# Attention, then two feed-forward layers: the attention's side work is laid into idle times behind its plan, and the change-over to the first layer is regrouped

## The chip, the cores and the metric

The kernel runs on one core of a Trainium2 chip. The metric is the device time of one execution in microseconds, the median of several runs. The engines are PE (TensorE, the matmuls), DVE (VectorE), ACT (ScalarE), POOL (GpSimd) and SP (SyncE, which here only issues DMAs). Each engine works through its own list of instructions in order, and waits on semaphores for the others.

## What is computed

```python
q_rot, k_rot = (rotate(q), rotate(k))          # rope; q, k, v: 4 batches, 8 heads, 576 tokens, 64
scores = scale * np.matmul(q_rot, k_rot.transpose(0, 1, 3, 2))
scores = scores - np.max(scores, axis=-1, keepdims=True)
attn = np.exp(scores)
attn = attn / (np.sum(attn, axis=-1, keepdims=True) + 1e-09)
x = np.matmul(attn, v)                          # -> 2304 tokens x 512
...
g = x @ w_gate                                  # MoE 1: 512 -> 1536
silu = g * (1.0 / (1.0 + np.exp(-g)))
val = x @ w_val
x = silu * val @ w_out                          # 1536 -> 512
...
h = x @ w_in                                    # MoE 2: 512 -> 2048
r = np.maximum(h, 0.0)
g = r * r
return g @ w_out                                # 2048 -> 512
```

## The kernel before

**Arithmetic.** Where full precision is wanted, an operand is split into a rounded high part and the remainder (two tiles or halves of a tile, `h` and `l`), and a product is three matmuls. The split is one ACT copy and one subtraction by DVE or POOL. The four batches' outputs x are 512 + 64 tokens each. MoE 1 does batches in pairs in the manner of Strassen: seven products of sums of blocks instead of eight. The sums of x blocks are called words (T1 to T4 are sums of two or more blocks, the others are plain x), and the sums of weight blocks are weight words.

**Attention** (up to some 355 us). 16 pairs of heads (4 batches, 4 pairs). For each: loads of q and k (`rot<-in_q_dram`), rope on DVE and POOL, copies to the layout of the heads (`kh`, `qa`, `qz` `<-rot`), scores `s` and their softmax (`nm`, `p`), transposes `pt` with copies `pc`, `av`, and then the output tile `xs`, which is split into `x0h`, `x0l` to `x3h`, `x3l` (one pair of names for each batch). Beside these lie *fillers*: the first two of MoE 1's chunks of ff columns for batches 0 to 2 (weights `w`, products `mm`, then `ys<-mm` by ACT and a store to `ypart` in DRAM).

The order of the attention is found by `Plan`: each operation is entered with its engine, its cost, a rank and what it reads and writes; a greedy loop with a clock of its own gives each engine that comes free the ready operation of the lowest rank. A tag has so many places, and an operation that begins a new buffer of the tag waits for a place. DMAs are operations on SP, with these two constants for when they land (ns, and bytes per ns):

```python
    LAND = 2000
    RATE = 310
```

In the plan lie also the spills (`xfull<-xs`, and `xsp<-x0h` and so on: the split x), and `add_words`: for the four words T1 to T4 of the first pair of batches it loads x back (`h<-xfull`, `wa<-xfull`), makes the sums (L777 and L778), stores them (`xsums`), loads each back (`h<-xsums`), splits it (L784 ACT, L785 POOL), and stores both halves (`xsum`).

**The change-over** (some 355 to 450 us). The order of everything after the attention is made by a second planner, `Order`, in stages. Stage 0 holds batch 3's part of the first two chunks (`q<-x3h`, L1064; then the 64 token rests of all batches, `xrh`, `xrd`, loaded by `accr<-xfull`), `down_first` (its products with `w_out`, `d<-h`, whose results go by `ys` and `yh` to `ypart[3]`), and the first weight words and x words of the steady state. `combine` loads raw weights, unpacks them (ACT, then three DVE instructions for each piece), adds them, and stores the words to `w1d` for later; `fetch_in` loads words stored before (`f<-w1d`), and `split_in` splits `f` into `wi`. The x words come by `xc<-xsp` and `xc<-xsum`. All of these DMAs are issued by SP.

Stage 1 is laid over the space of the attention's pools (`early.close()`); its tiles `cp`, `thr`, `th` are the copies by which ACT takes a product out of PSUM (`q` and `d`).

```python
    for o, ps, t in down_first(B - 1, hl):
        ys = new("ys")
        copy(ys, ps, 512, [t], [ys])
        dma(lambda o=o: ypart[B - 1][:, o, :], lambda ys=ys: ys(), [ys], [(ypd[B - 1], o)], 262144)
```

**Steady state** (from 450 us on). Two pairs of batches through MoE 1 and then MoE 2, PE busy nearly throughout; the change does not touch its code.

## Time and profile before

| | |
|---|---|
| median of 3 runs | 1140.83 us (1140.17 to 1141.53) |
| the profiled execution | 1141.04 us, its span 1139.3 us, mean granted clock 0.988 |
| PE | 1072.8 us busy (94%), 6126 matmuls |
| DVE, POOL, ACT | 738.2 us (65%), 703.8 us (62%), 612.1 us (54%) |
| DMA | 201.34 MB, mean 177 GB/s |

The busy time of an engine is the sum over its instructions. The span less PE's busy time, 66.5 us, is the time in which PE has nothing to do. Windows give the same by stretches of the program; the waits say for each engine who ended its idle times. In the timeline, the bracket behind an instruction is the idle time of its engine before it and who ended that. A granted clock of 1.00 is 2.4 GHz on PE.

### The profile page before, as it was taken

Reading aid. Unit: us, or ns where it says so; the run is one execution under the profiler, and the core shown is the slowest. Engines: PE = TensorE matmul, PEld = TensorE weight load, DVE = VectorE, ACT = ScalarE, POOL = GpSimd, SP = SyncE. Lnnn points to the kernel's source line nnn. Section 1 sums busy time; section 2 is a strip of 40 time slices with the busy share of each in tenths; the row PEclk is TensorE's granted clock in tenths of the full one; section 3 lists DMA queues with packets and bytes.
Section 4 is the critical chain, followed back from the end, with each engine's and each line's share of the span. In section 5 each row is a group of like instructions: output and inputs, shape, how many; then the busy total and the mean of one; then the engine's idle time right before and its main releaser. Section 6 shows DMA issues by size and latency. Waiting matters only on the chain.

```text
span 1139.3 us, 17496 instructions
## 1 busy us (share of the span) xinstructions
PE 1072.8 (94%) x6126; PEld 891.7 (78%) x6126; DVE 738.2 (65%) x1198; ACT 612.1 (54%) x1257; POOL 703.8 (62%) x596
## 2 busy tenths in 40 slices
PE   4898998999996949999999999999999999999998
PEld 3687787787884837888888888888888888788886
DVE  8676877666762617778866676575777756255454
ACT  7666767675652513654564455736554454553432
POOL 6877676678111505678858666785666669475651
PEclk9999999999999979999999999999999999999999
DMA  9876678899514753576668555454343435412102
GB/s 304 229 211 178 190 211 256 243 289 269 153 65 150 273 235 95 186 246 219 237 243 267 194 171 195 141 201 143 126 143 125 171 126 166 152 61 84 29 18 74
DMA packets 100824, 201.34 MB, mean 177 GB/s; under 512 B 17280, under 2 KB 43648, under 8 KB 100736
## 3 DMA queue, kind: packets, MB, share of 16 engines
q1 hardware_dynamic: 100048, 199.50, 54.3%
q8 instruction: 48, 0.79, 0.3%
q10 hardware_dynamic: 688, 0.72, 0.2%
q14 instruction: 40, 0.33, 0.1%
HBM read 116.98 MB, written 61.08 MB: 156 GB/s over the span
## 4 chain that ended last, share of the span: by engine, by line
PE 79%; DMA 9%; DVE 3%; SPq 3%; POOL 2%; ACT 2%; issue 1%; ACTq 0%; DVEq 0%; POOLq 0%
PE d L1064 36%; PE q L1064 26%; PE s L656 5%; PE av L719 5%; PE pt L685 4%; PE mm L820 3%; DMA qa<-rot 2%; DMA xc<-xsum 2%; DMA ypart<-ys 1%; SPq L636 1%; DMA v<-in_v_dram 1%; DMA h<-xfull 1%; POOL rot L566 1%; DVE nm L662 1%; DMA ypart<-yh 1%
## 5 line engine op out<-in xcount | busy, mean ns | idle before, releaser
L1064 PE MATMUL q<-xc,wi 128*128 128x512 f32 x1296 | 310.5, 392 | 16.7 <-ACT cp L930 16.2
L1064 PEld LDWEIGHTS q<-xc,wi 128*128 128x128 f32 x1296 | 242.5, 189 | 69.3 <-ACT cp L930 17.5
L915 POOL TENSOR_TENSOR wi<-f,wi 128x512 fp32r<-128x512 f32 (+1 forms) x144 | 167.1, 1176 | 70.2 <-ACT wi L914 64.5
L1064 PE MATMUL d<-wo,h 128*128 128x512 f32 (+1 forms) x870 | 199.9, 388 | 0.3 <-POOL h L915 0.3
L915 POOL TENSOR_TENSOR h<-th,h 128x512 fp32r<-128x512 f32 x104 | 136.2, 1336 | 101.0 <-ACT h L914 99.9
L1064 PEld LDWEIGHTS d<-wo,h 128*128 128x128 f32 x870 | 162.1, 188 | 34.8 <-POOL h L915 1.2
L919 DVE TENSOR_TENSOR acc<-d,acc 128x512 f32<-128x512 f32 (+1 forms) x193 | 132.1, 688 | 71.1 <-PE d L1064 66.8
L1064 PE MATMUL d<-h,wo 128*128 128x512 f32 (+1 forms) x600 | 126.1, 369 | 2.7 <-ACT wo L914 1.1
L656 PE MATMUL s<-kh,qa 128*128 128x288 f32 x320 | 104.2, 351 | 24.8 <-DVE qa L614 12.0
L1064 PEld LDWEIGHTS d<-h,wo 128*128 128x128 f32 x600 | 104.6, 188 | 23.1 <-POOL wo L915 1.6
L662 DVE TENSOR_REDUCE nm<-s 128x1 f32<-128x576 f32 x144 | 106.2, 751 | 23.5 <-PE s L656 22.4
L664 ACT ACTIVATE p<-s,nm 128x576 f32<-128x576 f32 x144 | 105.8, 736 | 27.1 <-DVE nm L662 24.7
L685 PE MATMUL pt<-ident,p 128*128 128x128 f32 (+1 forms) x720 | 109.5, 275 | 7.8 <-ACT pc L677 3.9
L915 POOL TENSOR_TENSOR wo<-wf,wo 128x512 fp32r<-128x512 f32 x52 | 68.0, 1307 | 78.9 <-ACT wo L914 41.4
L930 ACT ACTIVATE cp<-q 128x512 f32<-128x512 f32 x108 | 64.6, 599 | 83.5 <-PE q L1064 82.6
L914 ACT ACTIVATE wi<-f 128x512 fp32r<-128x512 f32 (+1 forms) x144 | 79.7, 572 | 49.2 <-POOL f L922 26.9
L685 PEld LDWEIGHTS pt<-ident,p 128*128 128x128 f32 (+1 forms) x720 | 85.9, 135 | 15.4 <-ACT pc L677 5.7
L919 DVE TENSOR_TENSOR q<-q,cp 128x512 f32<-128x512 f32 x36 | 25.2, 699 | 105.5 <-PE q L1064 104.5
L656 PEld LDWEIGHTS s<-kh,qa 128*128 128x128 f32 x320 | 61.3, 197 | 39.3 <-ACT p L664 20.2
L656 PE MATMUL s<-kl,qz 128*128 128x288 f32 x288 | 85.3, 304 | 0.0
L914 ACT ACTIVATE wo<-wf 128x512 fp32r<-128x512 f32 x52 | 32.9, 633 | 83.3 <-PE d L1064 70.2
L719 PE MATMUL av<-pc,v 128*64 128x256 f32 x640 | 77.5, 389 | 0.0
(167 smaller groups left out, 1837.7 us busy)
## 6 DMA issues: line engine op xcount, KB each, us to landing
raw<-in_moe_w_out_dram SPq DMA_DIRECT2D x26, 512.0 KB, 3.8
w1d<-f SPq DMA_DIRECT2D x10, 896.0 KB, 5.0
f<-w1d SPq DMA_DIRECT2D x10, 896.0 KB, 5.7
f<-w2d SPq DMA_DIRECT2D x10, 896.0 KB, 4.5
rot<-in_k_dram SPq DMA_DIRECT2D x15, 576.0 KB, 5.2
rot<-in_q_dram SPq DMA_DIRECT2D x15, 576.0 KB, 5.1
kh<-rot SPq DMA_DIRECT2D x60, 144.0 KB, 3.0
raw<-in_moe_w_in_dram SPq DMA_DIRECT2D x16, 512.0 KB, 4.0
```

Of the source, the lines that this page charges most:

```text
L566: (2 * w, lambda en, x=x, c0=c0, c1=c1, tab=cs if i else csq: en.tensor_tensor(out=x()[:, :, c0:c1], in0=x()[:, :, c0:c1], in1=tab()[:, :, ...
L656: nc.tensor.matmul(ps()[:, i, :HS], lhsT=a, rhs=w, start=y == 0, stop=y == len(prods) - 1)
L662: plan.add("DVE", 755, lambda ps=ps, nm=nm: nc.vector.tensor_reduce(out=nm(), in_=ps()[:, :, :HS], axis=AX.XY, op=ALU.max, negate=True), [ ...
L664: plan.add("ACT", 930, lambda x=x, ps=ps, nm=nm, p=p: nc.scalar.activation(p().rearrange("p (a b) -> p a b", a=2), ps()[:, :, :HS], AF.Exp ...
L685: nc.tensor.matmul(pt()[:kk, off + n * 128:off + n * 128 + 128], lhsT=p()[:, c * 128:c * 128 + kk], rhs=ident, is_transpose=True)
L719: nc.tensor.matmul(av()[h * 64:h * 64 + 64, 0:256], lhsT=vt()[:, h, c], rhs=pcs[c]()[:, h * 256:h * 256 + 256], start=c == 0, stop=c == 4)
L820: nc.tensor.matmul(ps()[:, :n], lhsT=x(), rhs=y(), start=f, stop=l), rd + (rdi[i] if rdi else []), [ps], rank[0], cols=n)
L914: od.add(("ACT", act(n, 205), lambda: nc.scalar.activation(hi(), src(), AF.Copy)), rd, [whi])
L915: sub = lambda e: lambda: e.tensor_tensor(out=lo(), in0=src(), in1=hi().bitcast(F32), op=ALU.subtract)
L919: od.add(("DVE", dve(n), lambda: nc.vector.tensor_tensor(out=out(), in0=a(), in1=b(), op=op)), rd, wr)
L930: od.add(("ACT", act(n), lambda: nc.scalar.activation(out(), src(), func, scale=scale)), rd, wr)
L1064: nc.tensor.matmul(ps(), lhsT=x, rhs=y, start=first and i == 0, stop=last and i == 2, skip_group_check=True)
```

## The change

- **A plan and a second pass.** Operations entered while `plan.extra` is set are left out of the greedy loop and of its rings. When the greedy plan is finished, `fill` goes through them in the order of entry and gives each the first time at which its engine (and, for a DMA, a model of the DMA engines) has an idle time of its length; then all operations are sorted by time. Extra are the `xfull` spills, the `xsp` spills of batches 2 and 3, the words and the first weights.
- **Words.** They use `rot` buffers, after the last load of q and k; the sums are stored once, unsplit (`xsum`, half the size), and are split at the change-over: one load of 512 KB for a word instead of two, and one ACT and one DVE or POOL instruction for each half.
- **First weights.** The gate and value weights of the steady state's first step are unpacked in the attention, in halves of 128 columns: `add_first` makes eight loads of 256 KB into the one buffer `wa`, one ACT and three DVE instructions on 256 columns for each, 16 additions on 128 columns, and four stores `w1d<-wf` of 448 KB in pieces of 256 bytes. The change-over loads the words (`fetch_in`).
- **Spills.** The upper two of batch 3's four pairs are spilled as `xsp`, no longer the lower two (1 MB less).
- **`ys`** has two buffers in the attention instead of one.
- **The `ypart[3]` stores** of `ys` and `yh` are issued from ACT's queue.
- **Places.** The tiles of stages 0 and 1 are allocated in another order, in one schedule.

```diff
     def order(self):
...
+        base = [i for i, o in enumerate(ops) if not o["extra"]]
...
-        return [ops[i]["fn"] for i in out]
+        return [ops[i]["fn"] for i in self.fill(out, taken)]
+
+    def fill(self, out, taken):
...
+        for i, o in enumerate(ops):
+            if not o["extra"]:
+                continue
+            t = max([ops[j]["done"] + self.HOP for j in o["deps"]], default=0)
...
+            for eng, ns, fn in o["ways"]:
+                names = [eng]
+                a = room(names, t, ns)
+                if o["size"]:
+                    while True:
+                        m = room(["DMA"], a + self.LAND, o["size"] / self.RATE)
+                        c = room(names, max(a, m - self.LAND), ns)
...
+        return sorted(out + [i for i, o in enumerate(ops) if o["extra"]], key=lambda i: ops[i]["at"])
...
+            plan.extra = b > 1
+            for i in range(2 if b != 3 or j >= HK else 0):
...
-            wa, h, v = buf("wa", [128, 512], U32, 1, tp0), buf("h", [128, 2, 512], F32R, 4, hp0), buf("h", [128, 2, 512], F32R, 4, hp0)
+            h, v = buf("rot", [128, 2, S], bufs=QB), buf("rot", [128, 2, S], bufs=QB)
...
-            for n in range(4):
-                t = buf("h", [128, 2, 512], F32R, 4, hp0)
-                plan.add("SP", 450, lambda n=n, t=t: nc.sync.dma_start(out=raw(t()[:, 0]), in_=xsums[n][:, i]), [(xsummed, (n, i))], [(t, 0)], at + 4, size=262144)
...
+        def add_unpack(src, dst, wr, at):
+            rw, p = buf("wa", [128, 512], U32, 1, tp0), buf("wp", [128, 256], U32)
...
+            plan.add("SP", 500, lambda: load_raw(src, rw()), [(wbuf[NW - 1][2], 1)], [(rw, 0), (rw, 1)], at, size=262144)
...
+        def add_first(i, n):
...
+            dst = lambda: wfirst[i].rearrange("p a (k b) -> p a k b", k=2)[:, :, :, n * 64:n * 64 + 64]
+            plan.add("SP", 450, lambda: nc.sync.dma_start(out=dst(), in_=f()[:, 1:].bitcast(F32)), [(f, x) for x in (0, 1, 4, 5, 6, 7)], [], at, size=458752)
...
-                ps, ys = buf("mm", [128, 512], pool=pp), buf("ys", [128, 512], pool=tp0)
+                ps, ys = buf("mm", [128, 512], pool=pp), buf("ys", [128, 512], F32, YS, tp0)
...
-        dma(lambda o=o: ypart[B - 1][:, o, :], lambda ys=ys: ys(), [ys], [(ypd[B - 1], o)], 262144)
+        od.add(("ACT", 100, lambda o=o, ys=ys: nc.scalar.dma_start(out=ypart[B - 1][:, o, :], in_=ys())), [ys], [(ypd[B - 1], o)], size=262144)
...
-    wg = split_in(combine(w_gate, NW, w1d[0][0]))
-    wv = split_in(combine(w_val, NW, w1d[0][1]))
+    wg, wv = (split_in(fetch_in(keep)) for keep in w1d[0])
...
-        for h in range(2):
...
+        x = xc[word]
+        dma(lambda x=x: x()[:, 1].bitcast(F32), lambda word=word: xsum[(T1, T2, T3, T4).index(word)], [], [(x, (1, i)) for i in range(HK)], 524288, hold=True)
+        for i in range(HK):
+            split(lambda x=x, i=i: x()[:, 0, i], lambda x=x, i=i: x()[:, 1, i], lambda x=x, i=i: x()[:, 1, i].bitcast(F32), 512, [(x, (1, i))], (x, (0, i)), (x, (1, i)), True)
```

**PE at the end of the attention.** The rows of before, from the last transposes of the softmax to the first product of batch 3 (`mm` are the fillers, `av` the last attention product, `q` the first product of batch 3; line numbers of before and of the changed file differ):

```order
L741 MATMUL pt<-ident,rb 128x128 x2
L719 MATMUL av<-pc,v_126 64x256 x8
L719 MATMUL av<-pc_123,v_126 64x256 x2
L722 MATMUL av<-pcr,v_126 64x64 x10
L820 MATMUL mm<-h,w 128x512 x6
L741 MATMUL pt<-ident,rb 128x128 x2
L820 MATMUL mm<-h,w 128x512 x18
L1064 MATMUL q_4789<-x3h,w 128x512
```

The same place in the changed kernel:

```order
L924 MATMUL mm<-h,w 128x512 x2
L765 MATMUL pt<-ident,p 64x128
L924 MATMUL mm<-h,w 128x512 x4
L821 MATMUL pt<-ident,rb 128x128 x2
L799 MATMUL av<-pc,v_124 64x256 x8
L799 MATMUL av<-pc_121,v_124 64x256 x2
L802 MATMUL av<-pcr,v_124 64x64 x10
L924 MATMUL mm<-h,w 128x512 x6
L821 MATMUL pt<-ident,rb 128x128 x2
L1173 MATMUL q_4825<-x3h,w 128x512
```

Of the 24 `mm` matmuls that stood behind the last `av`, six stand there now; the others stand ahead of it, among and before the `pt` transposes.

**ACT at the change-over.** Before, from the last copies of batch 3's part to the first copies of the x words' products (`thr` and `cp`):

```order
L930 ACTIVATE accr_4785<-d_4797 128x256
L914 ACTIVATE wi_4767<-f_4777 128x512
L930 ACTIVATE yh<-d_4798 128x512
L914 ACTIVATE wi_4767<-f_4777 128x512
L930 ACTIVATE thr_5104<-d_4795 128x256
L930 ACTIVATE thr_5105<-d_4796 128x256
L930 ACTIVATE cp_5065<-q_4791 128x512
L930 ACTIVATE cp_5066<-q_4789 128x512
```

And in the changed kernel:

```order
L1039 ACTIVATE accr_4812<-d_4834 128x256
L1039 ACTIVATE accr_4812<-d_4831 128x256
L1369 DMA ypart_83<-ys 128x512 x2
L1039 ACTIVATE accr_4812<-d_4832 128x256
L1369 DMA ypart_83<-ys 128x512
L1039 ACTIVATE accr_4812<-d_4833 128x256
L1023 ACTIVATE xc_4790<-xc_4790 128x512 x2
L1039 ACTIVATE yh<-d_4834 128x512
L1369 DMA ypart_83<-yh 128x512
L1039 ACTIVATE thr_5091<-d_4831 128x256
L1039 ACTIVATE thr_5092<-d_4832 128x256
L1039 ACTIVATE cp_5084<-q_4827 128x512
```

The DMA rows of `ypart_83` are new on ACT, and so is the split of a word (`xc_4790`); the splits of the weights (`wi`) have moved elsewhere. On SP the corresponding rows are those of before:

```order
L911 DMA w1d_4709<-f_4776 128x1792
L911 DMA ypart_83<-ys 128x512
L390 DMA raw_4771<-in_moe_w_out_dram 128x1024
L911 DMA ypart_83<-ys 128x512 x2
L390 DMA raw_4772<-in_moe_w_out_dram 128x1024
L911 DMA acc_5081<-ypart_81 128x512
```

**SP at the change-over.** In the changed kernel, from the last stores of the attention to the first loads of the change-over (`w1d_89` and `w1d_90` are the first weights' words, `xfull_88` is batch 3's x):

```order
L952 DMA ypart_82<-ys 128x512 x2
L890 DMA w1d_90<-wf 1792x1x64
L952 DMA ypart_82<-ys 128x512
L843 DMA xfull_88<-xs 128x576
L846 DMA xsp_101<-x3h 128x512
L846 DMA xsp_102<-x3l 128x512
L1020 DMA f_4820<-w1d_89 128x1792
L1020 DMA accr_4812<-xfull_85 128x4x64
L1020 DMA accr_4812<-xfull_86 128x4x64
L1020 DMA accr_4812<-xfull_87 128x4x64
L1020 DMA accr_4812<-xfull_88 128x4x64
L1020 DMA f_4821<-w1d_90 128x1792
```

The loads of raw weights are gone from this place, the loads `f<-w1d` have come in, the first of them ahead of `accr`, and the last store of the first weights stands five rows ahead of it.

**ACT in the attention.** One of the eight places of the new unpacking (`wa<-wa`; `p` is the softmax, `pc` a copy of the transposes that `av` reads):

```order
L808 ACTIVATE rs<-sums_139 128x4
L744 ACTIVATE p,sums_139<-s,nm 128x576
L810 ACTIVATE rb<-rs 128x256
L871 ACTIVATE wa<-wa 128x256
L757 ACTIVATE pc<-pt 128x512
L744 ACTIVATE p,sums_139<-s,nm 128x576
```

The row `wa<-wa` waits for a load and stands ahead of softmax work; there is no such row in the kernel before.

## Rows read from the trace of the kernel before

**Rows 1.** Windows: busy us (instructions) of each engine, granted clock, DMA share, GB/s.

```profile
...
80.00:180.00 100.00, 94.54 (x778) 77.95 (x776) 75.97 (x132) 66.71 (x162) 69.33 (x48) 0.98 0.69 196
180.00:210.00 30.00, 24.37 (x182) 19.50 (x179) 21.91 (x33) 19.67 (x49) 19.88 (x12) 0.96 0.81 249
210.00:355.00 145.00, 141.85 (x1155) 116.49 (x1153) 94.89 (x176) 86.65 (x209) 70.05 (x57) 1.00 0.63 189
355.00:378.00 23.00, 14.55 (x54) 10.99 (x55) 4.80 (x9) 4.87 (x9) 2.72 (x3) 0.93 0.52 151
378.00:397.00 19.00, 19.00 (x128) 17.51 (x127) 13.81 (x23) 11.66 (x24) 13.68 (x13) 1.00 1.01 372
397.00:415.00 18.00, 3.66 (x20) 2.82 (x18) 0.00 (x0) 0.04 (x1) 0.60 (x1) 0.74 1.02 401
...
425.00:450.00 25.00, 22.21 (x105) 17.38 (x104) 16.60 (x28) 9.73 (x18) 10.35 (x9) 1.00 0.29 85
450.00:1139.30 689.30, 683.70 (x3244) 572.86 (x3242) 444.05 (x686) 350.59 (x645) 454.58 (x405) 1.00 0.46 155
```

**Rows 2.** Waits of PE, 354.5 to 450: us in total, times, longest.

```profile
PE q L1064 <- ACT cp L930: 15.5, 1, 15.5
PE mm L820 <- ACT ys L847: 4.9, 3, 2.8
PE q L1064 <- ACT ys L847: 4.0, 1, 4.0
```

**Rows 3.** Timeline of PE: start, us, instruction, idle time before it.

```profile
362.73 1.66 PE L820 MATMUL mm<-h,w 128*128 128x512 f32 x6 [2.81 <-ACT ys L847]
368.42 0.79 PE L1064 MATMUL q<-x3h,w 128*128 128x512 f32 x1 [4.03 <-ACT ys L847]
```

**Rows 4.** Chain that ended last, 352 to 450: start, us, what.

```profile
363.43 4.24 DMA ypart<-ys
...
368.42 4.39 PE q L1064 x12
...
397.35 9.66 DMA ypart<-ys
407.07 7.78 DMA ypart<-yh
...
416.16 5.77 PE q L1064 x18
...
423.28 2.73 PE q L1064 x12
```

**Rows 5.** Timeline of all engines, 397 to 417.

```profile
397.75 2.91 PE L1064 MATMUL q<-xc,wi 128*128 128x512 f32 x12
...
414.96 0.66 ACT L930 ACTIVATE thr<-d 128x256 f32<-128x256 f32 x2 [18.72 <-DMA ypart<-yh]
```

**Rows 6.** Timeline of SP's queue: start and us of the four issues.

```profile
359.71 3.62 SPq L911 DMA_DIRECT2D accr<-xfull  x4
```

**Rows 7.** Tile h, 170 to 260: its engine sat idle until (us, times).

```profile
  DMA h<-xfull: 6.2, 2
  DMA wa<-xfull: 2.2, 1
```

**Rows 8.** DMA issues: count, KB of one, median us to landing; to 355, then after.

```profile
h<-xfull SPq DMA_DIRECT2D x6, 256.0 KB, 4.3
...
w1d<-f SPq DMA_DIRECT2D x2, 896.0 KB, 9.7
...
accr<-xfull SPq DMA_DIRECT2D x4, 128.0 KB, 5.5
...
xfull<-xs SPq DMA_DIRECT2D x1, 288.0 KB, 2.6
```

**Rows 9.** Groups of ACT and of DVE on 256 columns: busy us, mean ns.

```profile
L914 ACT ACTIVATE wi<-f 128x256 fp32r<-128x256 f32 x4 | 1.7, 414 | 0.8 <-DVE f L927 0.8
...
L927 DVE SCALAR_TENSOR_TENSOR t<-t,q 128x256 f32<-128x256 f32 x4 | 1.7, 417 | 1.3 <-ACT t L930 1.1 <-PE q L1064 0.2
```

More of the change, by code (lines that the diff above doesn't have):

```diff
@@ L1 @@
+import bisect
 import heapq
@@ L31 @@
 NFB = 3
+YS = 2
 NW = G0
@@ L119, in make_ready @@
                 heapq.heappush(ready[eng][ops[i]["mode"]], (ops[i]["rank"], i))
-        for i in range(len(ops)):
+        for i in base:
             if not left[i]:
@@ L143, in order @@
                         left[j] -= 1
-                        if not left[j]:
+                        if not left[j] and not ops[j]["extra"]:
                             eng = ops[i]["eng"]
@@ L156, in order @@
                     new = [b for b in ops[i]["bufs"] if b not in placed and b.tag in ring]
-                    short = [b.tag for b in new if ring[b.tag][0] is not None]
+                    short = [b.tag for n, b in enumerate(new) if ring[b.tag][sum(x.tag == b.tag for x in new[:n])] is not None]
                     if short:
@@ L183, in order @@
                         hold = moved - now - ns
+                        ops[i]["moved"] = moved
+                    ops[i]["ns"], ops[i]["done"] = ns, now + ns + max(hold, 0)
+                    for b in new:
+                        taken.setdefault(b.tag, []).append(b)
                     out.append(i)
@@ L186, in order, with room @@
                     at(now + ns + hold, "done", i)
-        assert len(out) == len(ops), "the plan is stuck"
+        assert len(out) == len(base), "the plan is stuck"
         self.end = now
-        return [ops[i]["fn"] for i in out]
+        return [ops[i]["fn"] for i in self.fill(out, taken)]
+    def fill(self, out, taken):
+        ops, gap = self.ops, 60
+        busy = {e: [] for e in ("DVE", "ACT", "Pool", "SP", "DMA")}
+        for i in out:
+            o = ops[i]
+            if o["eng"] in busy:
+                busy[o["eng"]].append((o["at"], o["at"] + o["ns"]))
+            if o["size"]:
+                busy["DMA"].append((o["moved"] - o["size"] / self.RATE, o["moved"]))
+        def room(names, t, ns):
+            while True:
+                was = t
+                for e in names:
+                    k = max(0, bisect.bisect_right(busy[e], (t, 1e12)) - 1)
+                    while k < len(busy[e]) and busy[e][k][0] < t + ns + gap:
+                        if busy[e][k][1] > t:
+                            t = busy[e][k][1]
+                        k += 1
+                if t == was:
+                    return t
+        ends, start, free = {}, {}, {}
+        for o in ops:
+            if "done" in o:
+                for b in o["bufs"]:
+                    ends[b] = max(ends.get(b, 0), o["done"])
+                    start[b] = min(start.get(b, 1e12), o["at"])
+        limit = {b: start[c] for tag, was in taken.items() for b, c in zip(was, was[self.places[tag]:])}
+        for i, o in enumerate(ops):
+            if not o["extra"]:
+                continue
+            t = max([ops[j]["done"] + self.HOP for j in o["deps"]], default=0)
+            for b in o["bufs"]:
+                if b.tag in self.places and b not in ends and b not in free:
+                    was = taken.setdefault(b.tag, [])
+                    n = self.places[b.tag]
+                    free[b] = max(start.get(was[-1], 0) if was else 0, ends[was[-n]] + self.HOP if len(was) >= n else 0)
+                    was.append(b)
+                t = max(t, free.get(b, 0))
+            best = None
+            for eng, ns, fn in o["ways"]:
+                names = [eng]
+                a = room(names, t, ns)
+                if o["size"]:
+                    while True:
+                        m = room(["DMA"], a + self.LAND, o["size"] / self.RATE)
+                        c = room(names, max(a, m - self.LAND), ns)
+                        if c == a:
+                            break
+                        a = c
+                if best is None or a < best[0]:
+                    best = a, eng, ns, fn
+            a, o["eng"], o["ns"], o["fn"] = best
+            if a > min([limit[b] for b in o["bufs"] if b in limit], default=1e12) - 2000:
+                a = t
+            o["at"], o["done"] = a, a + o["ns"]
+            bisect.insort(busy[o["eng"]], (a, o["done"]))
+            if o["size"]:
+                m = a + self.LAND
+                bisect.insort(busy["DMA"], (m, m + o["size"] / self.RATE))
+                o["done"] = m + o["size"] / self.RATE
+            for b in o["bufs"]:
+                start.setdefault(b, a)
+                ends[b] = max(ends.get(b, 0), o["done"])
+        self.done = max(o["done"] for o in ops)
+        return sorted(out + [i for i, o in enumerate(ops) if o["extra"]], key=lambda i: ops[i]["at"])
@@ L769, in add_words @@
+        xspilled = Buf(None, None)
+        half = S // 2
         def add_words(i):
             at = 1000 + i
-            wa, h, v = buf("wa", [128, 512], U32, 1, tp0), buf("h", [128, 2, 512], F32R, 4, hp0), buf("h", [128, 2, 512], F32R, 4, hp0)
-            b12, b11, b22, b21 = (lambda: wa().bitcast(F32)), (lambda: raw(h()[:, 0])), (lambda: raw(h()[:, 1])), (lambda: raw(v()[:, 0]))
-            for ap, b, k, key in ((b12, 1, i, wa), (b11, 0, i, (h, 0)), (b22, 1, HK + i, (h, 1)), (b21, 0, HK + i, (v, 0))):
-                plan.add("SP", 450, lambda ap=ap, b=b, k=k: nc.sync.dma_start(out=ap(), in_=xfull[b][:, k, 0:NM]), [(xspilled, b * NP + k)], [key], at, size=262144)
@@ L864, in tile_attention_moe_moe2 @@
             add_filler(b)
+        plan.extra = True
+        for i in range(2):
+            for n in range(2):
+                add_first(i, n)
         for i in range(HK):
```

90 lines of the change are left out of this document (57 added, 33 removed).

## The prediction

> **What bounds the kernel now.** The windows come first, since the program has stages with different limits. Over the last 689 us TensorE (PE) is busy for 683.7, so that stretch offers at most 5.6 us [rows 1], and the order of the steps on PE there is nearly the same before and after. What can be won lies ahead of 450 us. There the windows show three places where PE is idle: the attention after 80 us (5.46, 5.63 and 3.15 us in the three windows from 80 to 355, so 14.2 together), the stretch 355 to 378, where it works 14.55 of 23 us, and 397 to 415, where it works 3.66 of 18. PE is the bound of the attention nearly everywhere, and in the two other places it waits for somebody. The chain of waits on PE between 354.5 and 450 names him [rows 2]: a copy `cp` by ScalarE (ACT), once, 15.5 us; `ys` copies by ACT, 4.9 and 4.0; and the window 425 to 450 holds another 2.8 us of idle time [rows 1], small waits for the first `wo` and `acc`.
>
> Why is ACT late? PE's own rows at the end of the attention show three groups of six filler matmuls and then the first `q`, each behind a `ys` copy, the last two with 2.81 and 4.03 us idle [rows 3], 8.9 in all [rows 2]. There is one `ys` buffer, so each copy waits until the store of the one before has landed; the chain that ended last goes through such stores, the second one 4.24 us [rows 4]. The 15.5 us are the same thing at a larger scale: ACT stands 18.72 us before `thr` and waits for the store `ypart<-yh` to land, because `thr` lies where `yh` lies; the `cp` copies that PE needs stand behind it in ACT's order [rows 5]. That store is late because it is issued on SP at 407.07 and takes 7.78 us to land, and it stands behind `ypart<-ys`, issued at 397.35 (9.66 us) behind the loads of the x words [rows 4]. In that burst the DMA engines are full: share 1.01, 372 GB/s [rows 1].
>
> **The change, part by part.**
>
> *Two `ys` buffers, and a plan without the spills.* In the new order 18 of the 24 filler matmuls that stood behind the last `av` stand ahead of it, among the transposes of the attention, and only six are left. That PE work is the same wherever it is; only its idle time counts. Of the 8.9 us one dependence is left: the last attention output goes through transpose, `xs` and its split before the first `q`. A group of six takes 1.66 us, which covers most of that; I leave 0.7, nearer to nothing than to the 2.81 of a group that waited. **-8.2**. The twelve `q` after the idle time take 4.39 us where twelve later take 2.73 [rows 4]; the granted clock of 355 to 378 is 0.93 [rows 1], so between the levels 2.4 and 1.2 GHz. With PE busy before them I give those back: **-1.6**.
>
> *The ACT stall.* `thr` and `cp` get places of their own, which no store still reads. The `ypart<-ys` stores and `ypart<-yh` are issued from ACT's own queue. The stall of 15.5 us has no cause left: **-15.5**. The 18 `q` matmuls after it take 5.77 us; at 2.73 for 12 they take 4.1: **-1.7** [rows 4]. The condition is that the x words are there. PE has 29.3 us of work from its first `q` at 368.42 to the first one on `xc` at 397.75 [rows 4, 5]. In the new order SP issues two `f<-w1d` (1.8 MB), `accr` (0.5 MB) and ten `xc` loads (5.2 MB): 7.6 MB, at 372 to 401 GB/s [rows 1] some 19 to 20 us, beginning some 4 us after the first `q` (the last `xfull` store, which lands after 2.6, [rows 8], and a few issues), and a landing ends some 2 us behind. That is 26 us against 29.3: a margin of about 3. What is no longer there: the unpacking of the first weights (4 ACT, 20 DVE instructions), 2 MB of raw weights, 1.8 MB of `w1d` stores, and 2 MB of the doubled `xsum`; in their place eight halves of `xsum` are split again by ACT and DVE or GpSimd, under PE work, and an ACT split of one half on 512 columns can't be longer than two on 256 of 0.41 [rows 9].
>
> *What comes late next.* SP puts a whole `f<-w1d` ahead of the four `accr<-xfull` loads, which landed 5.5 us after their issue and whose issues took 3.62 us [rows 6, 8]. ACT's split `xrd<-accr` needs them, and now stands ahead of the copy `t` which frees the `q` tile for PE. If PE is there first it waits: at least 0, at most the issues plus the landing less the work of PE that hides them (from 12 `q` on), some 5.5. I take **+2.5**. The `w_out` raw loads are issued earlier by the two weights that need not be unpacked, which should end most of the 2.8 us of 425 to 450: **-2.0** (bounds 0 and -2.8).
>
> *The attention.* Between 180 and 210 the words are made in the middle of the greedy plan. GpSimd and VectorE (DVE) stand in front of their loads for 6.2 and 2.2 us, 8.4 together [rows 7], and PE is idle for 5.63 of that stretch [rows 1]: about 0.67 us of PE for one us of such waits. The words move to the end, behind the last load of q and k, lose their second pass (8 ACT splits, 8 GpSimd subtractions, 6 MB of DMA), and 1 MB of spills goes. **-5.6** if nothing of that comes back. In their place come eight loads of 256 KB with one ACT and three DVE instructions each (about 0.41 for 256 columns, [rows 9]), 16 additions on 128 columns, and four stores of 448 KB. That is 3.3 us of ACT and 10 of DVE in 275 us, in which DVE works 193 and ACT 173 [rows 1], so the work itself has room. The waits are what counts: the planner reckons a landing at 2 us plus the size over 310 GB/s, 2.85 for 256 KB, while the row says 4.3 for `h<-xfull` [rows 8]. So each of these eight loads and the two words' lists find an engine standing some 1.3 us in front of data, in order, with softmax work behind it: 10 times 1.3, 13 us of waits, at 0.67 some 8.7. The lower bound is nothing, since they are laid into idle times. I take the middle, **+4.3**. The plan of the attention without these steps could win more of the other 8 us or lose some; I take 0, with bounds of -6 and +5.
>
> One store is unlike all others: `w1d<-wf` goes out in pieces of 256 bytes. The nearest rows are `accr<-xfull` in the same pieces (128 KB, 5.5 us) and `w1d<-f` in large ones (896 KB, 9.7 in the burst) [rows 8]; so 448 KB lie between 5 and 3.5 times 5.5, 19 us. All but the last have time. The last one stands on SP five rows ahead of the first `f<-w1d`, and the second `f<-w1d`, behind `accr`, reads it: at 5 us it is covered; at 19, SP stands in front of that load with the `xc` loads behind, some 9 us late against a margin of 3. The Trainium skill, "DMA: Bandwidth & Descriptors", Specifications, asks for 512 bytes at least for the full rate; the slow `accr` rows agree with it, and by it the upper end would be the right one, a stall of about 6.
>
> **The sum.** -8.2 -1.6 -15.5 -1.7 +2.5 -2.0 -5.6 +4.3 = -27.8. The profiled execution took 1141.04 for a span of 1139.3, 0.2 above the median of 1140.83; so 1140.8 - 27.8 = **1113**.
>
> **The rivals.**
> 1. *The waits at the change-over come back in part.* For it: stores and loads share the DMA engines, share 1.02 in 397 to 415 [rows 1]; a store on ACT's queue stands in ACT's order too, and the margin is 3 us. If the burst or the last `w1d` store is late by the 9.7 us that `ypart<-ys` took to land, PE stands about 6 to 10 us: 1113 + 8 = 1121. Against: no copy waits for a landing any more. The Trainium skill, "DMA: Bandwidth & Descriptors", "Issuing engines are not separate DMA queues", says that another issuing engine saves only the time of issuing; the rows agree that the landing (7.78 us) was what was long. Chance 0.17.
> 2. *The added steps disturb the attention more.* SP, ACT and DVE go in order; `wa` is one buffer, so SP can stand before a load with `kh` and `qa` behind it. Two stretches like 180 to 210 (5.63 idle, and 1.2 of clock at 0.96, so 13.7) instead of the 4.3: 1113 + 9 = 1122. Chance 0.17.
> 3. *The attention closes up.* If its idle share falls to that of 210 to 355 (3.15 of 145 us, so 6.0 of 275 instead of 13.8 without the tail's first 0.4: -7.8 where the sum has -1.3) and `accr` costs nothing: 1113 - 6.5 - 2.5 = 1104. For it: the greedy plan no longer places spills. Chance 0.13.
> 4. *Slower.* The one mechanism: a `wa` load waits on SP for DVE's last read of the buffer, and `kh`/`qa` of the next pair wait behind it. The eight loads would have to cost PE 3.5 us each on top to use up the 28; the whole stretch 180 to 210 cost 5.63. At 4 us each: 1113 + 32 = 1145, chance 0.02.
>
> **Chances and range.** My forecast, 1113 within 1107 to 1118: 0.51. The range takes in most of rivals 1 to 3: 1102 to 1126. No change can be told within 0.2%, 2.3 us, about what a measurement of this kernel can tell: 0.01. Slower 0.02, faster 0.97.
>
> **What would show it.** Right: `ypart<-ys` gone from PE's waits around the last `av`, with under 1.5 us before the first `q`; no wait of ACT for a `ypart` store; PE busy through what was 397 to 415; a wait of `q` for ACT `t` of up to 5 us ten us after the first `q`; some 36 to 40 us of idle PE in all instead of 66.5; waits of DVE and ACT for `wa` of 1 to 2 us each. Wrong: waits of PE for `xc`, `f` or `cp` around 25 to 35 us after the first `q` (rival 1); idle PE of over 20 us between 80 us and the last `av` (rival 2), or under 8 (rival 3).

## The result, and the profile of the changed kernel

The changed kernel takes 1100.55 us (1098.68 to 1102.60, four runs) against 1140.50 for the one before (1138.49 to 1141.53, four runs): a ratio of 0.9652, 95% interval 0.963 to 0.967, so about 40 us or 3.5% faster. The forecast was 1113, its range began at 1102; the result lies 1.5 us below the range. The profiled execution took 1100.28 us for a span of 1098.5.

The windows of the changed kernel, to be laid beside [rows 1] (its first `q` comes at 346.28):

```profile
80.00:180.00 100.00, 95.39 (x792) 78.87 (x791) 76.30 (x136) 68.59 (x167) 70.92 (x50) 1.00 0.68 195
180.00:210.00 30.00, 29.00 (x229) 24.58 (x227) 24.08 (x41) 19.75 (x49) 21.75 (x14) 1.00 0.76 225
210.00:340.00 130.00, 128.53 (x1034) 106.30 (x1032) 101.09 (x185) 83.01 (x201) 71.61 (x66) 1.00 0.66 191
340.00:355.00 15.00, 14.39 (x92) 11.23 (x91) 3.29 (x7) 2.10 (x5) 1.67 (x2) 1.00 0.75 221
355.00:450.00 95.00, 92.86 (x492) 80.41 (x491) 70.67 (x110) 53.60 (x103) 62.98 (x61) 0.98 0.65 221
450.00:1098.50 648.50, 643.25 (x3031) 537.63 (x3029) 409.87 (x629) 323.87 (x600) 415.66 (x364) 1.00 0.45 151
```

PE was idle for 5.46 and 5.63 us in the first two of these windows before; it is idle for 4.61 and 1.00 now, and its granted clock, 0.98 and 0.96 there before, is 1.00. Between 355 and 450, where the two long gaps stood, 2.14 us of idle time are left. The waits of PE from 340 to 450 are two rows, where [rows 2] had 24.4 us in its three:

```profile
PE q L1173 <- DVE t L1036: 2.1, 1, 2.1
PE q L1173 <- ACT xrh L829: 0.6, 1, 0.6
```

The end of the attention on PE, which answers to [rows 3]:

```profile
343.12 0.75 PE L802 MATMUL av<-pcr,v 128*64 128x64 f32 x20
343.80 1.66 PE L924 MATMUL mm<-h,w 128*128 128x512 f32 x6
...
346.28 0.47 PE L1173 MATMUL q<-x3h,w 128*128 128x512 f32 x1 [0.61 <-ACT xrh L829]
```

No row of it waits for a `ys` copy; 0.61 us before the first `q` is what the dependence through `xs` and `xrh` leaves. And ACT at the place of [rows 5], with the stores now among its own rows:

```profile
372.61 0.84 ACTq L1369 DMA_DIRECT2D ypart<-ys  x2
...
376.07 0.33 ACTq L1369 DMA_DIRECT2D ypart<-yh  x1
376.85 0.38 ACT L1039 ACTIVATE thr<-d 128x256 f32<-128x256 f32 x1 [0.81 <-PE d L1173]
...
379.65 0.60 ACT L1039 ACTIVATE cp<-q 128x512 f32<-128x512 f32 x1 [1.00 <-PE q L1173]
```

`thr` waits 0.81 us for PE and for no store. The chain that ended last shows what the 2.1 us of `q` behind `t` are:

```profile
346.58 2.54 DMA xfull<-xs
349.20 0.32 SPq L1020
...
351.71 5.17 DMA accr<-xfull
...
357.21 1.44 DVE accr L1031
358.67 0.64 ACT xrd L1023
...
360.31 0.61 DVE t L1036
```

The `xfull` store of the last pair lands, SP issues `f<-w1d` and then `accr`, which lands after 5.17 us; DVE and ACT prepare the rests, and only then comes the `t` that PE's next `q` needs.

From 15 us to the first `q`, two rows of before and one of the changed kernel (the row from 80 us on stands in the first experiment):

```profile
15.00:80.00 65.00, 57.74 (x437) 47.06 (x439) 50.68 (x87) 47.31 (x114) 55.24 (x37) 0.97 0.85 242
80.00:368.42 288.42, 265.73 (x2128) 217.09 (x2124) 193.24 (x340) 174.96 (x422) 160.97 (x118) 0.99 0.68 200
```

```profile
15.00:80.00 65.00, 57.26 (x460) 47.16 (x461) 52.34 (x88) 47.72 (x116) 55.32 (x37) 1.00 0.84 241
```

By place, the span became shorter by 40.8 us in the profiled executions. The tail's waits went from 8.9 us to 0.6, the stall from 15.5 to nothing, the waits for `wo` and `acc` from 2.8 to nothing, and 2.1 us came in behind `accr`: together -24.5, where the forecast had -23.2. From 15 us to the first `q`, without the tail, idle time went from 21.1 us to 14.8 (7.26 + 13.8 to 7.74 + 7.07), and the busy time for the same matmuls from 323.5 to 315.9, with the clock at 1.00 in these rows: -13.9, where the forecast had -1.3. (Of the 7.6 us of busy time about one can be the execution's: a second profiled execution of the changed kernel had 316.9.) The rest, some -2.4, is nearly all busy time from the first `q` on, 747.0 before and 744.8 now.

### The profile page after: what moved, and what is told of

The parts are those of the page before. It is cut to its first block, busy times and chain, and to the rows that moved or that the text cites. A ratio compares the mean times of both kernels' runs of the same rounds, so it can differ in the third digit from the quotient of the medians.

```text
span 1098.5 us, 17488 instructions
## 1 busy us (share of the span) xinstructions
PE 1063.0 (97%) x6126; PEld 888.1 (81%) x6126; DVE 748.4 (68%) x1212; ACT 608.7 (55%) x1258; POOL 706.8 (64%) x605
## 4 chain that ended last, share of the span: by engine, by line
PE 84%; DMA 6%; DVE 4%; ACT 2%; POOL 2%; SPq 2%; issue 1%; ACTq 0%; DVEq 0%; POOLq 0%
PE d L1173 38%; PE q L1173 26%; PE s L736 6%; PE av L799 5%; PE pt L765 5%; PE mm L924 4%; POOL rot L646 1%; SPq L716 1%; DMA wf<-o2d 1%; ACT p L744 1%; DVE th L1036 1%; PE av L802 1%; DVE nm L742 0%; PE pt L821 0%; DMA qz<-rot 0%
## 5 line engine op out<-in xcount | busy, mean ns | idle before, releaser
L736 PE MATMUL s<-kh,qa 128*128 128x288 f32 x320 | 103.7, 349 | 21.1 <-DVE qa L694 12.5
L742 DVE TENSOR_REDUCE nm<-s 128x1 f32<-128x576 f32 x144 | 105.8, 751 | 13.9 <-PE s L736 11.7
L744 ACT ACTIVATE p<-s,nm 128x576 f32<-128x576 f32 x144 | 105.5, 734 | 16.8 <-DVE nm L742 14.8
L1023 ACT ACTIVATE wi<-f 128x512 fp32r<-128x512 f32 (+1 forms) x144 | 78.5, 570 | 38.1 <-POOL f L1031 15.9
L736 PEld LDWEIGHTS s<-kh,qa 128*128 128x128 f32 x320 | 59.7, 193 | 34.1 <-ACT p L744 13.9
L759 DVE COPY pc<-pt 128x512 f32<-128x512 f32 (+1 forms) x95 | 63.9, 685 | 20.3 <-PE pt L765 19.9
```

The costliest lines, as they stand in the source:

```text
L736: nc.tensor.matmul(ps()[:, i, :HS], lhsT=a, rhs=w, start=y == 0, stop=y == len(prods) - 1)
L742: plan.add("DVE", 755, lambda ps=ps, nm=nm: nc.vector.tensor_reduce(out=nm(), in_=ps()[:, :, :HS], axis=AX.XY, op=ALU.max, negate=True), [ ...
L744: plan.add("ACT", 930, lambda x=x, ps=ps, nm=nm, p=p: nc.scalar.activation(p().rearrange("p (a b) -> p a b", a=2), ps()[:, :, :HS], AF.Exp ...
L759: nc.vector.tensor_copy(dst()[:kk], pt()[:kk, :n])
L1023: od.add(("ACT", act(n, 205), lambda: nc.scalar.activation(hi(), src(), AF.Copy)), rd, [whi])
```

## The experiments

Three questions: which part of the change shortened the attention, what ended the stall behind `thr`, and what the added unpacking costs. Each kernel below is the changed one with one edit, unless it says otherwise; "idle" is PE's idle time between 80 us and the first `q` in the profiled execution, 7.7 us in the changed kernel. The kernel before took 1140.5 to 1143.0 us (medians) beside these kernels, so differences of one to three microseconds between two kernels are at the edge of what can be told.

### Everything in the greedy plan again

```diff
-            plan.extra = True
+            plan.extra = False
...
-            plan.extra = b > 1
+            plan.extra = False
...
-        plan.extra = True
+        plan.extra = False
```

> The changed kernel with every step in the greedy plan again (nothing marked extra): spills, words and first weights compete by their ranks. If the attention's gain of some 12 us comes from planning the main work alone, it goes back by 6 to 12: 1107 to 1113 us. If it comes from the work that the words no longer do and from their late place, the attention keeps it: 1100 to 1103. If part of it was only the granted clock of the profiled execution of before (0.97 and 0.98 in its windows up to 210), the clock of this one's windows shows 1.00 or not without regard to the order.

1111.2 us (1110.6 to 1113.5), idle 17.7 us. One row for each of the two kernels, from 80 us to its first `q`, says where it went, first with everything planned and then the changed kernel:

```profile
80.00:362.48 282.48, 264.75 (x2097) 215.82 (x2095) 203.33 (x343) 184.58 (x447) 157.18 (x121) 0.98 0.64 185
```

```profile
80.00:346.28 266.28, 258.60 (x2102) 213.78 (x2101) 203.06 (x363) 172.68 (x418) 164.28 (x129) 1.00 0.68 195
```

10.0 us more of idle time, and 6.2 more of busy time for the same work at a clock of 0.98 instead of 1.00. These 16.2 us are more than the difference of the medians, 10.6: from the first `q` on this kernel is 3.0 us shorter than the changed one (749.2 against 752.2), and its profiled execution was the slowest of the four. The words' smaller work and their late place (`rot<-xfull` from 292 us on here, from 283 in the changed kernel) are common to both kernels, so they are not what made the difference; the plan is. The miss of the forecast is of this size.

### Only the spills planned

The edit leaves out the `plan.extra` lines of `add_spill` alone.

> The changed kernel with the spills in the greedy plan again; words and first weights stay in the second pass. With everything in the plan the attention had 17.7 us of idle PE after 80 us instead of 7.7. If the spills, 46 stores on SP that the planner's order is built around, are what disturbs it, most of those 10 come back: 1106 to 1111 us. If it is the words or the first weights, 1100 to 1103.

1107.6 us (1103.6 to 1108.1), idle 14.1 us. The spills (44 stores in the trace, not 46) alone cost seven of the eleven microseconds. The end of the attention shows that two `ys` buffers do not end the tail by themselves:

```profile
352.84 1.66 PE L922 MATMUL mm<-h,w 128*128 128x512 f32 x6 [0.47 <-ACT ys L949]
355.24 1.64 PE L922 MATMUL mm<-h,w 128*128 128x512 f32 x6 [0.74 <-ACT ys L949]
357.61 0.50 PE L1171 MATMUL q<-x3h,w 128*128 128x512 f32 x1 [0.74 <-ACT ys L949]
```

With spills and words planned:

> The changed kernel with spills and words in the greedy plan and only the first weights in the second pass. If the words (waits of GpSimd and VectorE for their loads) do the harm: at least 3 us above the kernel with the spills alone planned. If the spills do it, or the first weights: equal to that one within 2 us.

1107.3 us (1106.6 to 1111.2), idle 15.9: equal to the one above within its runs, so the words add nothing that these runs can tell. With only the first weights planned:

> The changed kernel with only the first weights in the greedy plan, spills and words in the second pass. If the eight loads and their 32 instructions in the queues of ACT and VectorE are what the plan suffers from: 1105 to 1111 us. If not: 1099 to 1103.

1102.7 us (1099.9 to 1104.7), idle 10.5: two microseconds, at the edge of what can be told.

### By what the planned spills do harm

Two kernels differ from the one with only the spills planned in the spills' ranks, or in their size:

```diff
-... [(xspilled, g)], g + 1 + rk("sp", g), size=294912)
+... [(xspilled, g)], 800 + g, size=294912)
...
-... [], g + rk("sp", g), size=262144)
+... [], 800 + g, size=262144)
```

> As the kernel with only the spills planned (1107.6 us, 14.1 us of idle PE between 80 us and the first q), but with ranks behind everything else in the plan: the greedy loop still places them, whenever SP has nothing else ready. If their ranks are what pushes other loads back, the time falls to that of the second pass: 1100 to 1103. If placing them in the loop at all, with their claim on its modelled DMA rate, is the harm: 1105 to 1109.

```diff
-... [(xspilled, g)], g + 1 + rk("sp", g), size=294912)
+... [(xspilled, g)], g + 1 + rk("sp", g), hold=2950)
...
-... [], g + rk("sp", g), size=262144)
+... [], g + rk("sp", g), hold=2850)
```

> The spills planned at their old ranks, but without a size: they take their 450 ns of SP in the plan and keep their tile for 3 us, and put no load on its modelled DMA rate. If the model of the DMA rate is what moves the q and k loads and so the rope: 1100 to 1103 us. If the slot on SP and the tile's release are: 1105 to 1109.

With the late ranks 1099.8 us (1099.1 to 1100.5) and 8.6 us idle: as good as the second pass in time. (Its first `q` comes 3.4 us later than in the changed kernel, at 349.65, and PE loses next to nothing from there to 450, where the changed kernel has 2.1 us of idle time.) Without a size 1111.3 us (1107.8 to 1112.0), 16.7 us idle. So it is the ranks, and not the modelled DMA rate. On SP the order differs: with the old ranks the stores of a pair often stand among the `kh<-rot` copies of the next pair, with the late ones mostly behind them (in the changed kernel some `xsp` stores stand among them, too). SP's waits for `xs` in front of an `xfull` store were, with the old ranks, with the late ones, and in the changed kernel (us in total, times, longest):

```profile
SPq L842 <- DVE xs L823: 12.7, 7, 3.2
```

```profile
SPq L842 <- DVE xs L823: 4.2, 3, 2.8
```

```profile
SPq L843 <- DVE xs L823: 3.3, 2, 2.5
```

Behind such waits stand copies to `kh` and `qa`. That these waits are the way in which the ranks act is not shown: the kernel without sizes had 7.7 us of them and was the slowest.

Everything planned, but with those late ranks:

> The changed kernel with everything in the greedy plan, without a second pass, but the spills ranked behind the main work (words and first weights are so already). If ranks are all that the second pass changes: 1099 to 1102 us. If first weights and words in the loop still cost what separates the kernel with only the first weights planned (1102.7) from the changed one (1100.6): 1102 to 1105.

1106.0 us (1103.0 to 1107.4), idle 14.0 us: better than 1111.2 and worse than the second pass. With the spills out of the way, words and first weights in the greedy loop still cost some 5 us, though their ranks are behind all others there, too. So a late rank was enough for the spills, but not for all side work. Nor do SP's waits for `xs` go with the times: here, and in the kernel with spills and words planned (1107.3 us), they were:

```profile
SPq L843 <- DVE xs L823: 15.3, 6, 7.2
```

```profile
SPq L842 <- DVE xs L823: 37.9, 9, 15.9
```

Shown is that placing side work in the greedy loop costs the time, and that for the spills it is their ranks; by which engine's waits it reaches PE stays open.

### The kernel before with the second pass

The new `Plan` in the kernel before, spills and words marked extra; nothing else is changed.

> The kernel before with only the second pass: the spills and the words are left out of the greedy plan and laid into idle times; one ys buffer, words with their second pass, unpacking and stores at the change-over as before. If the plan alone gives the attention's gain, it has 8 to 12 us less idle PE and lower clock loss before the first q, the 15.5 us stall stays: 1124 to 1132 us against 1140.5. If the attention's gain is due to the words' smaller work: 1136 to 1141.

1144.2 us (1142.0 to 1144.9, ten runs), ratio 1.0025 (1.0013 to 1.0037): slower than before by a hair, and neither theory had it. But the first `q` comes at 343.12 instead of 368.42, with 4.9 us idle ahead of it, tail included. The waits of PE after it:

```profile
PE q L1146 <- DVE t L1009: 27.8, 1, 27.8
PE q L1146 <- ACT cp L1012: 15.6, 1, 15.6
```

The 25 us that the plan gave are paid back in one wait. In this kernel the words use the fillers' `h` tiles, so the second pass can put them only behind the fillers' last `h` tiles: all but the first word load (`wa<-xfull`, 163.38) are issued from 318 to 368 us. Most of their sums, stores and splits then stand on SP and ACT at the change-over, among the loads that PE waits for:

```profile
ACT h L864 <- DMA h<-xsums: 19.7, 3, 18.2
ACT thr L1012 <- DMA ypart<-yh: 18.9, 1, 18.9
```

The stall behind `thr` is there as before. So the second pass needs the change in the words; whether their other buffers or their smaller work is not separated here.

### The second pass and the words alone

Back to one `ys` buffer, first weights unpacked at the change-over, old places of stage 1's tiles, and `ypart` stores on SP: of the change only the second pass, the lighter words in `rot`, the spill of 1 MB less, stage 0's places and the one schedule are left.

> The plan's second pass and the words in rot buffers alone: one ys buffer, first weights at the change-over, old places, stores on SP. If these two parts carry the change, the attention is as short as in the changed kernel (first q by 350), and the stall behind thr is back, but shorter than 15.5 us, since the burst has 4 MB less: 1103 to 1113 us. If all the parts are needed: 1115 to 1125.

1100.5 us (1099.8 to 1101.5), idle 5.4 us, as fast as the whole change. The 15.5 us did not come back: PE stands 2.1 us behind a `cp`. The stores stand on SP behind the loads of the x words again. But before the change SP still had nine DMAs to issue between the copy `yh` and its store, loads of `w_out` and `acc` among them, and stood 8.6 us for landings of earlier DMAs:

```profile
395.12 0.60 ACT L930 ACTIVATE yh<-d 128x512 f32<-128x512 f32 x1 [0.48 <-PE d L1064]
...
401.12 3.71 SPq L911 DMA_DIRECT2D acc<-ypart  x3
...
407.07 0.32 SPq L911 DMA_DIRECT2D ypart<-yh  x1
```

Here the store goes out when the copy is done:

```profile
367.74 2.89 SPq L1016 DMA_DIRECT2D ypart<-ys  x3
372.82 0.32 SPq L1016 DMA_DIRECT2D ypart<-yh  x1
```

```profile
372.19 0.60 ACT L1035 ACTIVATE yh<-d 128x512 f32<-128x512 f32 x1
...
378.18 1.15 ACT L1019 ACTIVATE wi<-f 128x512 fp32r<-128x512 f32 x2 [3.25 <-DVE f L1027]
...
380.19 0.66 ACT L1035 ACTIVATE thr<-d 128x256 f32<-128x256 f32 x2
```

`ypart<-yh` goes out 29.0 us after the first `q` (at 343.85), where it went out 38.7 us after it before [rows 4]; the copy `yh` itself came no earlier, 28.3 us after it against 26.7. The store took 7.2 us and had landed at 380.0, just before ACT reached `thr`, which waits for no store. ACT had stood 3.25 us for DVE's `f` ahead of it; without that wait `thr` would have waited some 3 us (an estimate from these rows), not 18.7.

### One buffer, one queue, the old places, each undone by itself

```diff
-YS = 2
+YS = 1
```

> The changed kernel with one ys buffer in the attention instead of two, as before, with the same memory laid out. If the second buffer is what let the fillers move ahead of the last av, the groups of six come back behind it with some 3 to 8 us of idle time in front of the first q: 1104 to 1110 us. If the plan without the spills did that by itself, at most one store is waited for: 1100 to 1103.

1103.4 us (1100.0 to 1104.2), between the two theories, idle 9.9 us, first `q` at 350.4. No wait for a store stands at the tail. The second buffer is worth at most some 3 us, in the attention, and the runs overlap those of the changed kernel. The tail was ended by the plan.

```diff
-        od.add(("ACT", 100, lambda o=o, ys=ys: nc.scalar.dma_start(out=ypart[B - 1][:, o, :], in_=ys())), [ys], [(ypd[B - 1], o)], size=262144)
+        dma(lambda o=o: ypart[B - 1][:, o, :], lambda ys=ys: ys(), [ys], [(ypd[B - 1], o)], 262144)
```

> The changed kernel with the ypart stores of batch 3 issued from SP again. If their own queue ended the 15.5 us stall, ACT waits again behind stores that stand behind the loads: 1108 to 1118 us. If the places of thr and cp ended it, no copy needs a store to have landed and the time stays: 1100 to 1102.

1101.2 us (1099.7 to 1105.8): no difference. The stall stays away without the own queue.

The third puts `cp`, `tw`, `acc`, `h`, `th`, `thr`, `wf`, `wo` back into the old order, with the stores on ACT:

> The changed kernel with stage 1's tiles in the old order of allocation, so that thr lies again where a store still reads; the stores stay on ACT's queue. If the place makes the wait: ACT stands before thr until ypart<-yh has landed, 4 to 8 us after its issue, of which PE's twelve q hide some 3: 2 to 5 us of idle PE behind a cp, 1102 to 1106 us. If the wait came from the stores' late issue alone, it is gone on their own queue: 1100 to 1102.

1108.0 us (1106.6 to 1109.5), more than either theory had. ACT's rows show two waits, and PE stands behind both:

```profile
380.74 0.99 ACTq L1369 DMA_DIRECT2D ypart<-ys  x2
381.77 0.38 ACT L1039 ACTIVATE accr<-d 128x256 f32<-128x256 f32 x1 [5.35 <-DMA acc<-ypart]
...
387.97 0.66 ACT L1039 ACTIVATE thr<-d 128x256 f32<-128x256 f32 x2 [3.63 <-DMA ypart<-yh]
```

```profile
382.21 0.39 PE L1173 MATMUL d<-xrh,wi 128*128 128x256 f32 x1 [1.98 <-ACT accr L1039]
...
389.17 3.04 PE L1173 MATMUL q<-xc,wi 128*128 128x512 f32 x12 [2.54 <-ACT cp L1039]
```

ACT's two stores stood until a load of `acc` had landed, and with them the copies behind them, 5.35 us; then `thr` waited 3.63 for the store in its place. With the stores on SP and the same places (the section ahead) there was neither. So in this kernel stores on ACT's queue held ACT up, which was the first rival's mechanism; with the new places it doesn't happen in the changed kernel. The own queue or the new places in the kernel before, each alone, was not tried.

### The unpacking in the attention, and the order at the change-over

Without `add_first`, with `combine` at the change-over as before:

> The changed kernel with the first gate and value weights unpacked at the change-over again and not in the attention. If the added steps cost the attention what the forecast took (4.3 us), the attention is 4 us shorter and the change-over, with 2 MB more on its queue, some 2 to 5 longer: 1099 to 1102 us. If they cost the attention nothing, only the loss at the change-over shows: 1102 to 1106.

1098.1 us (1097.1 to 1098.8). The first `q` comes at 341.9 instead of 346.3, and the change-over then has 4.5 us of idle time instead of 2.1. The same kernel again:

> The kernel without the unpacking in the attention once more, beside the one above and with more rounds: 1097 to 1099 us, which would be 0.2% under the changed kernel's 1100.6; if it was the chip of that call, 1100 to 1101.

1099.6 us (1096.5 to 1101.7, six runs). The changed kernel itself once more:

> The changed kernel itself, for comparison on the same chip with the four below: 1100 to 1102 us, PE's granted clock 1.00 in every window up to 340.

1100.6 us (1100.3 to 1102.2); the clock was not 1.00 in every window, but 0.97 between 15 and 80 us. So the unpacking costs the attention 1.5 to 4.4 us (first `q` at 344.7 and 341.9 without it), at most what was forecast, and saves 2.9 us from the first `q` on (752.2 us against 755.1 in both executions without it); without it the kernel is at best 1 to 2 us faster, which the overlapping runs don't settle. With the loads in another order:

> The changed kernel with the two loads f<-w1d held back until they are due, so that the four accr loads go first. The 2.1 us in which q waits for a copy behind accr should go: 1098 to 1099.5 us. Rival: the second f<-w1d, now behind five x words, comes late for the first product on xc: 1101 to 1106.

1099.9 us (1099.3 to 1101.2); the waits of `q` behind `t` are still 2.0 us, in two pieces, since `accr` reads what the last `xfull` store writes, whatever stands between. No difference that can be told. The same without the unpacking:

> First weights at the change-over (as in the kernel without the unpacking in the attention, 1098.1 us), and their raw loads held back until due, so that accr goes first. If the 1.0 us of q behind t and the 2.1 behind cp come from the loads' order: 1095 to 1097.5 us. Rival: the weights are late for the first product on xc, 1099 to 1103.

1104.2 us (1102.2 to 1106.0), above the rival's range, with 7.4 us idle at the change-over: the first `q` on `xc` waits 4.2 us for a `cp` that stands on ACT behind the split of the late weights.

### The kernel before with late ranks for half its spills

> The kernel before with one thing changed: the spills of batches 2 and 3 get ranks behind everything else of the plan but the words (those of batches 0 and 1 keep theirs, since the words wait for them). If the spills' ranks alone hold the attention up, its second half and the tail close up by some 8 to 12 us, and the stall behind thr stays: 1126 to 1134 us. If the spills matter only beside the changed kernel's words and buffers: 1138 to 1142.

1143.0 us (1137.8 to 1146.4, ten runs), ratio 1.0017 (1.0000 to 1.0034). The order on PE did not change in a single row, and on SP the stores stand only a few rows later. So this doesn't tell whether the ranks by themselves would shorten the attention of the kernel before.

## Why the prediction was wrong, point by point

**What failed: the plan's term in the attention.** "The plan of the attention without these steps could win more of the other 8 us or lose some; I take 0, with bounds of -6 and +5." With everything planned the same kernel takes 1111.2 us, with side work behind the plan 1100.6, so the term is -10.6 and lies outside its bounds. By place in the profiled executions: from 15 us to the first `q`, without the tail, the kernel before took 344.5 us, the one with everything planned 346.2, the changed one 330.7. So the words and the added steps, for which the sum had -1.3, came to +1.7, and the plan to -15.5, of which some 3 come back behind the first `q`. Two things were missed in the term. It was bounded by PE's idle time in the attention alone, and the clock was left out: in the attention 7.6 of the 13.9 us came from busy time, at 1.00 where the rows had 0.98 and 0.96 [rows 1]. And the forecast looked for the side work's price in the waits of DVE and GpSimd in front of the words alone, though side work stood in SP's order, too, with waits of its own:

```profile
SPq L762 <- DVE xs L743: 8.0, 5, 2.4
...
SPq L780 <- DVE h L778: 4.8, 3, 3.2
```

Behind them stand loads and copies for the next pairs of heads. Whether it is by these waits that the plan loses its time is open, as said above: their totals don't go with the times. The third rival, 1104 us for an attention that closes up to the idle share of its second half, had the cause right, at a chance of 0.13, and its sign, under 8 us of idle PE between 80 us and the last `av`, stands in the trace; but even it had no clock in it, and it counted on nothing for `accr`.

**The words' stretch, -5.6, and the added steps, +4.3.** The stretch from 180 to 210 lost 4.6 of its 5.6 us of idle time. (The 8.4 us of waits behind the factor 0.67 are 3.6 of GpSimd and 4.8 of VectorE, not 6.2 and 2.2; the sum is right.) The added loads cost what was taken or less: without them the first `q` came 4.4 us earlier in one profiled execution, 1.5 in the other. The waits by which this was argued were fewer: 13 us were forecast (14.5 by the rows, since 4.3 less 2.85 is 1.45 and not 1.3), 6.4 stand in the trace for a landing of `wa` or of the words. So the size of +4.3 is in part luck. The waits in the changed kernel:

```profile
POOL rot L863 <- DMA rot<-xfull: 3.7, 2, 3.4
...
DVE wp L872 <- DMA wa<-in_moe_w_gate_dram: 1.3, 1, 1.3
...
ACT wa L871 <- DMA wa<-in_moe_w_val_dram: 0.7, 1, 0.7
DVE wp L872 <- DMA wa<-in_moe_w_val_dram: 0.7, 1, 0.7
```

**The tail, -8.2.** Measured -8.3. But two `ys` buffers are not its reason: with one the tail stayed away, and with two and planned spills 2.0 us of it came back.

**The stall, -15.5.** Measured -15.5, but the reason given, the own queue and the own places, is not needed: with neither it stayed away. The number is right by luck. What stood behind the stall was SP: before, `ypart<-yh` stood 11.4 us there behind the copy that it waits for, and 12.1 in the kernel before with the second pass; it went out at once in the two kernels without the stall whose stores were on SP. Whether SP was free by then because the burst was shorter (the words are loaded in one half) or because the store came ahead of the `acc` loads in the new order is not separated.

**The wait behind `accr`, +2.5.** Right in place and size, 2.1 us, but not by the reason given: with `accr` ahead of `f<-w1d` it was 2.0. `accr` waits for the landing of the last `xfull` store, and `f<-w1d` takes SP 0.32 us of that chain. **`wo`, -2.0:** all 2.8 went.

**The clock, -1.6 and -1.7.** Some 2.2 us of busy time went from the first `q` on, where these had 3.3; what was wrong was to look for the clock at the two long gaps alone.

**The store in pieces of 256 bytes.** Taken between 5 and 19 us; the four landed in 4.0 us at the median (3.8 to 6.9):

```profile
xsum<-rot SPq DMA_DIRECT2D x8, 256.0 KB, 3.5
...
w1d<-wf SPq DMA_DIRECT2D x4, 448.0 KB, 4.0
```

The Trainium skill, "DMA: Bandwidth & Descriptors", Specifications, which asks for 512 bytes at least for the full rate, would have had it near the upper end. The measurement decides: 448 KB in 4.0 us are near the 256 KB in 3.5 that `xsum<-rot` took in large pieces, so in these rows of the attention the small pieces show no cost. The section "Issuing engines are not separate DMA queues" of the same page of the Trainium skill says that DMAs from any engine run on the same DMA engines, and that several issuing engines save only the time of issuing. The runs agree: the stores from SP and from ACT made no difference in time (1101.2 and 1100.6 us).

## What to carry to other kernels

In a greedy planner, place side work that nobody waits for after the main work is placed: here that was worth 10.6 us of 1111. Ranking it behind the main work in the same loop was as good for the stores alone (1099.8), but not for all side work (1106.0). What the planner's order loses need not stand in the waits that look nearest to it: SP's waits for the stores did not go with the times. Buffers decide whether such work can be moved: in the kernel before, where the words share them with the main work, it was pushed to the end of the stage and paid for there in one wait. When a stall stands behind a store, look first at what the store's queue was busy with: here the stall stayed away without an own queue or own places for the stores, once nothing kept the store from going out behind its copy.

## What the runs showed of the hardware that was not expected

Idle time in short gaps came with longer busy time. Kernels with 14 to 18 us of idle PE between 80 us and the first `q` had 1066 to 1069 us of busy time for the same 6126 matmuls, those with 5 to 9 us, and no gap of over 3 us later, had 1063 to 1066: the granted clock was 0.98 or 0.99 in that stretch in the first and 1.00 in the second. The kernel with the old places is an exception, with 8.2 us, 0.99 and 1066.6. That the gaps make the clock fall is not shown by this, and not all of it is the kernel's: between 15 and 80 us the changed kernel had a granted clock of 1.00 in one profiled execution and 0.97 in another, with the same order of instructions and 7.74 and 6.85 us of idle time.
